# Two more token tiles kept in DRAM, and a fifth Strassen pair in the last stage of a fused attention and feed-forward kernel

## The chip, the cores and the metric

The kernel runs on one core of one Trainium2 chip. The metric is the device time of one execution in microseconds (us). A core has a matrix engine (PE, the tensor engine), a vector engine (VectorE, DVE in the profile), a scalar engine (ScalarE, ACT), GpSimd (POOL) and a queue engine (SP). PE reads from the on-chip memory SBUF and writes to PSUM, a small memory of eight banks that VectorE and ScalarE read. Transfers to and from DRAM are issued by SP, ACT and POOL, each in the order of its own queue. Every engine works through its queue in order, and waits at an instruction until the semaphores that it names have reached their values.

## The reference

```python
def _attn_ref(q, k, v):                      # q, k, v: 8 batches, 12 heads, 448 tokens, 64 wide
    scores = scale * np.matmul(q, k.transpose(0, 1, 3, 2))
    attn = np.maximum(scores, 0.0) ** 2 / S
    return np.matmul(attn, v)

def _moe_ref(x, g_ln, w_ch1, w_ch2):         # x: 8 batches, 448 tokens, 768 wide
    xn = (x - mu) / np.sqrt(var + 1e-06) * g_ln
    ch = np.maximum(xn @ w_ch1, 0.0) @ w_ch2   # 768 -> 3072 -> 768
    return x + ch
```

Scores are squared after the relu, not put through a softmax. The attention's output, with its heads side by side, is the x of the feed-forward part. The result is the residual x plus the second product, `ch`.

## The kernel before

**Pairs and stages.** The eight batches are taken two at a time: four pairs of 896 tokens, that is 7 tiles of 128 tokens each (t = 0 to 6). The code counts pairs from 0; this text calls them the first to the fourth, but keeps the code's number where it quotes the code. For each pair there is attention, a first product (768 to 3072, kept transposed in `hT`) and a second product (3072 to 768). The normalisation's scale per token (`rstd`) is applied behind the second product, which is linear in it.

The program alternates. The first product of pair p (`ffn1_pair`, `run`, L960) has PE to itself. Then comes a stretch in which the second product of pair p is mixed with the attention of pair p + 1. In the profile these mixed stretches are at about 100 to 175 us (pair 0's second product), 222 to 290 us (pair 1's, which this text calls the third pair's stretch where the attention in it belongs to the third pair) and 336 to 406 us (pair 2's; the fourth pair's stretch). The last stage, from 452 us, is pair 3's second product alone.

**Second product.** Directly (`ffn2`, L740), a tile takes 2 halves of 384 output columns x 24 matmuls = 48. By Strassen's scheme (`ffn2_pair`, L1099) two tiles of tokens, halves of the 3072 rows and halves of the 768 columns form 2 x 2 blocks, and 7 products of 12 matmuls do the work of 96. The sums of blocks of `h` are formed on VectorE (`h_sums_of`), the sums of blocks of `w2` (`t1`, `t3`, `t4`, `t6`, `t7`) on GpSimd and VectorE ahead of time. Pair 0 does 7 tiles directly. Pair 1 does 6 directly, in the order 0, 1, 2, 4, 5, 6, and keeps its middle tile, t = 3, in DRAM (`odd_out`, L789). Pair 2 does its own middle tile in `ffn2_mid` (48 matmuls) and three Strassen pairs, (0, 4), (1, 5) and (2, 6). Pair 3 does these three and a fourth, its middle tile with the one that pair 1 kept, which `odd_in` (L795) reads back into a free quarter of `w1`. The first Strassen pair of the last stage has a third PSUM bank (`third`), so that its products 4, 3 and 1 can start before the first product's last rows are there.

**The mixed stretches.** `interleave` (L13) runs a list of main units (parts of the second product: 6 matmuls each when direct) and a list of side units (attention), and spreads the second evenly over the first. A direct tile has 8 units, 4 for each half. The last part of a half calls `finish` (L754), which on VectorE (L756) takes the PSUM result, multiplies it by `rstd`, adds the residual tokens `xtok` (the buffer `xt_room`, one for all pairs) and writes one of three output buffers `o_room`. The store of one half is issued on SP (L776) when the next half finishes. Two units of pair 1 come ahead of the mixed list, and the last three behind the attention, so 43 of its 48 units are spread.

The side list (`attention`, L600) has 42 scores (6 groups of four heads x 7 blocks of 64 keys), three to a bundle: 14 bundles, one last value product, and two hooks. A score is 4 matmuls (L366), a relu on ScalarE (L377) into `attn_sb`, and a square, on VectorE (L381) or, for the third of a bundle in some stretches, on ScalarE (L379). There are three PSUM slots for scores and value products, and nine `attn_sb` buffers. The value product of a group (28 matmuls, L398) comes one or two bundles after the one with the group's last score, and VectorE scales it into `xT` (L404). After the last score of a group, SP issues the transposes of the keys and queries of the group three further on (L313, L318, L319), and POOL loads later ones.

The hook `even` stands tenth of the 17 side units. It issues on SP the fetches of the sums of `w1` that the next first product needs (L845), and, by the table `soon`, part of the transposes that put the next pair's attention output into `xt_room` as tokens:

```python
    soon = {(1, "even"): (0, 3, range(K1)), (2, "odd"): (0, 2, range(K1))}
```

that is, in pair 1's stretch token tiles 0 to 2, all 6 column blocks, one DMA transpose for each (`tokens_part`, L648). The remaining tiles, 3 to 6, follow beside the first product, in `between_two`.

**What orders it.** The program order is the order in which these Python functions run. A tracking layer places semaphores by it: a read of a buffer waits for the writes that stand ahead of it in the program, a write for the reads.

**Sums beside pair 1.** `beside_of` puts six VectorE additions (L1025, `t6` and `t7`) behind given main units.

Of the kernel before, what the change touches and what calls it, by code (L numbers as in the profile page):

```python
# [28 lines left out]
def kernel(  # L29
# [22 lines left out]
    nc = tc.nc  # L52
# [42 lines left out]
    odd_root = const.tile([P, 1], fp32)  # L95
# [162 lines left out]
    def transposes(b, m):  # L258
# [11 lines left out]
        if (b, m) == (0, 0):  # L270
# [5 lines left out]
            idle(32)  # L276
# [323 lines left out]
    def attention(bs, hooks):  # L600
# [25 lines left out]
        def bundle(items, at):  # L626
            for o, it in enumerate(items):
                item(*it, o == 2 and bs[0] in (by_dma, B - 2))
                if o == at:
                    product(it[0] - 1)  # L630
        units, due = [], [[]]
        for s in range(0, len(seq), 3):
            items = seq[s:s + 3]
            at = max((o for o, (n, i) in enumerate(items[:2]) if n > lo and i in (1, 2)), default=-1)
            units.append(lambda items=items, at=at: bundle(items, at))
# [149 lines left out]
    odd_kept = dram.tile([P, K2 + K1, P], bf16, name="odd_kept")  # L785
# [280 lines left out]
    def ffn2_mid(pair, a, b):  # L1066

        h = hT[pair].rearrange("p (kh k) s -> p kh k s", kh=2)[:, :, :, 3 * P:4 * P]  # L1070
        s, n = room0[:, :KH], KH - 1
        a, b = a[:, :DH], b[:, :DH]

        def rows(ps, left, name, lo, hi, first=False, last=False):
            for k in range(lo, hi):
                nc.tensor.matmul(ps, left[:, k], w2_sum[name][:, k], start=(first and k == lo),  # L1076
                                 stop=(last and k == hi - 1))

        def most(*at, **kw):
            rows(*at, 0, 6, **kw)  # L1080
            yield
            rows(*at, 6, n)
        yield from most(a, h[:, 1], "t4", first=True)
        nc.vector.tensor_add(s[:, :n], h[:, 0, :n], h[:, 1, :n])
        yield
        yield from most(b, h[:, 0], "t3", first=True)
        yield
        nc.vector.tensor_add(s[:, n], h[:, 0, n], h[:, 1, n])
        h_sums_of(pair, 0, "s1")
        for half, ps, left, name, then in ((0, a, h[:, 1], "t4", "t2"), (1, b, h[:, 0], "t3", "t5")):  # L1090
            if half:
                yield
            yield from most(ps, s, then)
            rows(ps, left, name, n, KH)
            rows(ps, s, then, n, KH, last=True)
            finish(pair, 3, half, 0, K1, ps, (nc.sync, nc.sync))
            h_sums_of(pair, 0, "s2", half * KQ * 2, (half + 1) * KQ * 2)

    def ffn2_pair(pair, t, ts, two_banks, z, last, third=None):  # L1099
# [3 lines left out]
        at, half = h_parts(pair, t), KH // 2  # L1103
# [20 lines left out]
        def result(ps, row, half):  # L1124
            p, u = (odd["pair"], MID) if t == MID and row else (pair, t + 4 * row)
            root = odd_root if p != pair else rstd[pair][:, u:u + 1]
            x = odd["x"] if p != pair else xtok[pair][:, :, u]
# [17 lines left out]
        else:  # L1145
# [20 lines left out]
            nc.vector.tensor_add(z, z, c)  # L1166
# [39 lines left out]
    def ffn2_units(pair):  # L1206
# [3 lines left out]
        if pair == 1:  # L1210
            then[order[-1]] = MID

        def unit(t, h, p):
            if h == 0 and p == 1 and t in then:
                statistics(pair, then[t])
# [200 lines left out]
```

## Time and profile before

| | us |
|---|---|
| median of 3 runs | 514.39 (514.38, 514.39, 516.76) |
| profiled execution | 513.95 |
| its span, first to last instruction | 512.2 |
| third pair's first product beside nothing else, 289.7 to 336.3 | 46.6, PE busy 46.6 |
| last stage, 459.2 to 512.2 | 53.0, PE busy 48.8, VectorE 33.8 |

| main groups by line | count | busy us |
|---|---|---|
| L745 second product, direct | 624 | 107.6 |
| L1114 second product, Strassen (all forms) | 588 | 103.6 |
| L1076 the middle tile of pair 2 | 48 | 9.0 |
| L377 relu of scores on ScalarE | 150 | 126.3 |
| L381 squares on VectorE | 98 | 60.0 |
| L379 squares on ScalarE | 28 | 26.6 |

A profile's span is the time from the first to the last instruction; the time of an execution is 1.75 us longer here. Busy times of PE overlap at the ends of matmuls (they are pipelined), so a group's mean duration is longer than the distance between its matmuls. "Idle before, releaser" is the time in which an engine had nothing to run and what ended it. SPq, ACTq and POOLq are the queues that issue transfers.

### The profile page before, as it was taken

Reading aid. Unit: us, or ns where it says so; the run is one execution under the profiler, and the core shown is the slowest. Engines: PE = TensorE matmul, PEld = TensorE weight load, DVE = VectorE, ACT = ScalarE, POOL = GpSimd, SP = SyncE. Lnnn points to the kernel's source line nnn. Section 1 sums busy time; section 2 is a strip of 40 time slices with the busy share of each in tenths; the row PEclk is TensorE's granted clock in tenths of the full one; section 3 lists DMA queues with packets and bytes.
Section 4 is the critical chain, followed back from the end, with each engine's and each line's share of the span. In section 5 each row is a group of like instructions: output and inputs, shape, how many; then the busy total and the mean of one; then the engine's idle time right before and its main releaser. Section 6 shows DMA issues by size and latency. Waiting matters only on the chain.

```text
span 512.2 us, 11457 instructions
## 1 busy us (share of the span) xinstructions
PE 504.7 (99%) x4559; PEld 299.7 (59%) x4559; DVE 385.0 (75%) x738; ACT 310.0 (61%) x513; POOL 130.3 (25%) x182
## 2 busy tenths in 40 slices
PE   8999999999999999999999999999999999999996
PEld 6677778955555555555555555555555555556663
DVE  4885755778787798858789968858887968868663
ACT  5966776588668266657757266639979366730000
POOL 8335102012402266321101099601100022200000
PEclk9999999999999999999999999999999999999999
DMA  9999999999979994329996999304997393322222
GB/s 198 206 207 206 210 206 157 157 149 211 167 134 193 173 226 139 129 66 175 186 234 111 196 177 185 93 11 79 185 193 174 75 219 117 94 77 63 63 61 61
DMA packets 124486, 76.31 MB, mean 149 GB/s; under 512 B 80562, under 2 KB 120498, under 8 KB 124434
## 3 DMA queue, kind: packets, MB, share of 16 engines
q1 hardware_dynamic: 93730, 41.38, 39.5%
q0 software_dynamic: 28544, 30.91, 37.4%
q10 hardware_dynamic: 2160, 3.31, 2.8%
q8 instruction: 35, 0.57, 0.5%
q14 instruction: 17, 0.14, 0.1%
HBM read 64.69 MB, written 17.89 MB: 161 GB/s over the span
## 4 chain that ended last, share of the span: by engine, by line
PE 95%; ACT 2%; DVE 2%; issue 0%; ACTq 0%
PE m_ps L903 28%; PE o_ps L745 19%; PE o_ps L1114 11%; PE m_ps L1114 8%; PE h_ps L686 8%; PE sc_ps L366 7%; PE av_ps L398 6%; PE h_ps L731 2%; ACT early L377 2%; PE h_ps L713 2%; PE o_ps L1076 2%; PE tr_ps L250 1%; PE idle_ps L236 1%; PE sum_ps L431 0%; DVE w L485 0%; ACT attn_sb L377 0%
## 5 line engine op out<-in xcount | busy, mean ns | idle before, releaser
L377 ACT ACTIVATE attn_sb<-sc_ps 128x896 bf16<-128x896 f32 (+4 forms) x150 | 126.3, 903 | 37.5 <-PE sc_ps L366 32.4
L907 ACT ACTIVATE hT_sb<-m_ps 128x448 bf16<-128x448 f32 x144 | 78.2, 543 | 52.1 <-PE m_ps L903 49.3
L745 PE MATMUL o_ps<-w,hT_sb 128*128 128x384 bf16 x624 | 107.6, 326 | 0.0
L745 PEld LDWEIGHTS <-hT_sb 128*128 128x128 bf16 x624 | 58.4, 98 | 46.0 <-issue 9.9
L381 DVE TENSOR_TENSOR attn_sb<-attn_sb 128x896 bf16<-128x896 bf16 x98 | 60.0, 622 | 25.0 <-ACT attn_sb L377 24.4
L686 PE MATMUL h_ps<-x_room,w 128*128 128x192 bf16 (+2 forms) x384 | 43.9, 263 | 0.0
L1114 PEld LDWEIGHTS <-hT_sb 128*128 128x128 bf16 x312 | 29.8, 98 | 22.0 <-issue 3.0
L985 DVE TENSOR_TENSOR m_ps<-x_room,m_ps 128x448 f32<-128x448 f32 x36 | 22.6, 628 | 21.6 <-ACT hT_sb L907 21.5
L686 PEld LDWEIGHTS <-w 128*128 128x128 bf16 x384 | 33.8, 97 | 6.9 <-issue 1.4
L903 PEld LDWEIGHTS <-w 128*128 128x128 bf16 x246 | 24.0, 97 | 22.8
L1114 PEld LDWEIGHTS <-x_room 128*128 128x128 bf16 x252 | 24.2, 98 | 17.3 <-issue 1.6
L404 DVE TENSOR_SCALAR xT_sb<-av_ps 128x896 bf16<-128x896 f32 (+2 forms) x30 | 27.0, 900 | 9.2 <-PE av_ps L398 8.9
L967 ACT COPY x_room<-m_ps 128x448 f32<-128x448 f32 x36 | 19.1, 531 | 21.2 <-PE m_ps L903 20.5
L903 PEld LDWEIGHTS <-w_sum 128*128 128x128 bf16 x210 | 20.5, 98 | 19.3 <-DVE w_sum L879 0.4
L159 POOL DMA_DIRECT2D k_sb<-in_k_dram x15 | 10.7, 713 | 79.6 <-DMA kT_sb<-k_sb 57.2
L159 POOL DMA_DIRECT2D v_sb<-in_v_dram x20 | 14.2, 710 | 58.6 <-PE sc_ps L366 44.2
L903 PE MATMUL m_ps<-x_sum,w 128*128 128x448 bf16 x120 | 29.1, 352 | 0.0
L663 DVE BATCH_NORM_STATS2 stats<-xtok_sb 128x6 f32<-128x384 bf16 x56 | 28.3, 547 | 0.9 <-DMA xtok_sb<-xT_sb 0.9
L366 PE MATMUL sc_ps<-qT_sb,kT_sb 64*64 64x448 bf16 x392 | 28.1, 358 | 0.2 <-ACT x_room L481 0.2
L485 DVE SCALAR_TENSOR_TENSOR w<-w,g_sb,x_room 128x512 bf16<-128x512 bf16 x36 | 25.6, 738 | 3.0 <-ACT x_room L481 3.0
L379 ACT ACTIVATE attn_sb<-attn_sb 128x896 bf16<-128x896 bf16 x28 | 26.6, 950 | 0.9
L398 PE MATMUL av_ps<-attn_sb,v_sb 64*64 64x448 bf16 (+2 forms) x532 | 26.1, 330 | 0.0
(196 smaller groups left out, 867.6 us busy)
## 6 DMA issues: line engine op xcount, KB each, us to landing
out_dram<-o_room SPq DMA_DIRECT2D x108, 96.0 KB, 2.5
w<-in_moe_w_ch_dram POOLq DMA_DIRECT2D x12, 384.0 KB, 14.1
w<-in_moe_w_ch_dram POOLq DMA_DIRECT2D x4, 1152.0 KB, 20.1
q_sb<-in_q_dram POOLq DMA_DIRECT2D x20, 224.0 KB, 5.9
v_sb<-in_v_dram POOLq DMA_DIRECT2D x20, 224.0 KB, 6.2
k_sb<-in_k_dram POOLq DMA_DIRECT2D x15, 224.0 KB, 5.3
kept<-room SPq DMA_DIRECT2D x4, 480.0 KB, 2.6
kept<-w_sum SPq DMA_DIRECT2D x16, 96.0 KB, 1.8
```

Source lines behind the costliest of these rows:

```text
L366: nc.tensor.matmul(ps[cols, r, o * w:(o + 1) * w], g["k"](i)[rows, cols], g["q"](i, r)[rows, blk[0]:sum(blk), cols], start=True, stop=True)
L377: nc.scalar.activation(a, ps[:, :, :len(slots) * w], ACTF.Relu)
L379: nc.scalar.activation(a, a, ACTF.Square)
L381: nc.vector.tensor_mul(a, a, a)
L398: nc.tensor.matmul(ps[cols, hh, :w], v_sb[rows, pr, j * D:(j + 1) * D], g["attn"][i][rows, r, :], start=(j == 0), stop=(j == J - 1))
L404: nc.vector.tensor_scalar_mul(x, ps[:, :, :w], score_scale)
L663: nc.vector.bn_stats(stats[:, n], xtok[pair][:, n * G:(n + 1) * G, t, :])
L686: nc.tensor.matmul(ps[:, :w + more], w1[:, c, ni * P:(ni + 1) * P], xc[b][:, c, s.start:s.stop + more], start=(c == 0), stop=(c == K1 - 1))
L745: nc.tensor.matmul(ps[:, :DH], hT[pair][:, ki, t * P:(t + 1) * P], w2[:, ki, cols], start=(o == 0), stop=(o == K2 - 1))
L903: nc.tensor.matmul(ps, *at, start=(first and c == 0), stop=(c == KQ - 1), skip_group_check=not first)
L907: nc.scalar.activation(hT[pair][:, n + KH * row, half * S:(half + 1) * S], ps, ACTF.Relu)
L1114: nc.tensor.matmul(ps, x[:, ki], y[ki] if isinstance(y, list) else y[:, ki], start=(first and ki == 0), stop=(ki == KH - 1), skip_group_ch ...
```

## The change

Two more tiles go the way of pair 1's middle tile. `LEFT` lists what is left to the last stage: of pair 1 the tiles 3 and 6, of pair 2 the tile 3. `odd_out` writes each, its `h` (24 x 128 columns) and its residual tokens, to a DRAM buffer of its own; `odd_roots` copies its `rstd` column. `odd_in` reads all three back in the last stage: into two free quarters of `w1` and into the `xT` of the last pair. Pair 1 now does five tiles directly: 0, 1, 2, 4, 5. `ffn2_mid` is gone; pair 2's stretch has the three Strassen pairs alone, the first with a third bank as in the last stage. Pair 3 has five Strassen pairs, the fifth made of pair 1's tile 6 and pair 2's tile 3. Further, which third scores of a bundle are squared on ScalarE is now given by `squares`: beside pair 0 all (as before), beside pair 1 those of every third bundle (before: none), beside pair 2 those of two bundles in three (before: all). The six additions beside pair 1 stand behind other units, and two idle matmuls at the start are left out. The table `soon` and the hooks are as before.

```diff
-            idle(32)
+            idle(30)
...
+        squares = {by_dma: (0, 1, 2), by_dma + 2: (0,), B - 2: (0, 1)}.get(bs[0], ())
+
-        def bundle(items, at):
+        def bundle(items, at, turn):
             for o, it in enumerate(items):
-                item(*it, o == 2 and bs[0] in (by_dma, B - 2))
+                item(*it, o == 2 and turn in squares)
...
+    LEFT = ((1, MID), (1, NT - 1), (2, MID))
...
     def odd_out(pair):
-        nc.gpsimd.dma_start(odd_kept[:, :K2], hT[pair][:, :, MID * P:(MID + 1) * P])
-        nc.gpsimd.dma_start(odd_kept[:, K2:], xt_room[:, :, MID])
-        odd["pair"] = pair
+        for i, (p, u) in enumerate(LEFT):
+            if p == pair:
+                nc.gpsimd.dma_start(odd_kept[i][:, :K2], hT[pair][:, :, u * P:(u + 1) * P])
+                nc.gpsimd.dma_start(odd_kept[i][:, K2:], xt_room[:, :, u])
...
     def odd_in():
-        t = w1[:, :KQ, :KH * P].rearrange("p c (k s) -> p c k s", s=P)
-        nc.sync.dma_start(t[:, :2].rearrange("p c k s -> p c (k s)"),
-                          odd_kept[:, :K2].rearrange("p (c k) s -> p c (k s)", c=2))
-        nc.sync.dma_start(t[:, 2, :K1], odd_kept[:, K2:])
-        odd["h"], odd["x"] = t[:, :2], t[:, 2, :K1]
+        x = xT[B // 2 - 1].rearrange("p c s -> p (c s)")[:, :(K2 + K1) * P].rearrange("p (c s) -> p c s", s=P)
+        for i, room in enumerate((w1[:, :KQ, :KH * P], w1[:, KQ:, KH * P:], None)):
...
+            nc.sync.dma_start(to.rearrange("p c k s -> p c (k s)"),
+                              odd_kept[i][:, :K2].rearrange("p (c k) s -> p c (k s)", c=2))
+            nc.sync.dma_start(odd[i]["x"], odd_kept[i][:, K2:])
...
     def h_parts(pair, t):
-        two = [h[:, :, :, t], odd["h"] if t == MID else h[:, :, :, t + 4]]
+        if t > MID:
+            two = [odd[1]["h"], odd[2]["h"]]
+        else:
+            two = [h[:, :, :, t], odd[0]["h"] if t == MID else h[:, :, :, t + 4]]
...
     def ffn2_units(pair):
-        order = [t for t in range(NT) if pair != 1 or t != MID]
-        then = dict(zip(order, order[1:]))
-        if pair == 1:
-            then[order[-1]] = MID
+        others = [u for p, u in LEFT if p == pair]
+        order = [t for t in range(NT) if t not in others]
+        then = {t: [u] for t, u in zip(order, order[1:])}
+        then[order[-1]] = others
...
     def strassen_units(pair, mm, banks, third=None):
         def all_of():
             end = pair == pairs - 1
-            if not end:
-                yield from ffn2_mid(pair, *mm)
-            for t in range(MID + end):
-                yield from ffn2_pair(pair, t, MID + end, banks(t), zs[t % 2], end and t == MID,
+            ts = MID + 2 * end
+            for t in range(ts):
+                yield from ffn2_pair(pair, t, ts, banks(t), zs[t % 2], end and t == ts - 1,
                                      third if t == 0 else None)
             yield
         g = all_of()
-        return [lambda: next(g)] * 4, [lambda: next(g)] * (4 + 3 * 14), g
+        return [lambda: next(g)] * 4, [lambda: next(g)] * (9 + 2 * 14), g
...
-            head, units, _ = strassen_units(pair, mm, lambda t: mm[::-1] if t % 2 else mm)
+            third = ps_m.tile([P, 512], fp32, tag="m", name="m_ps")
+            head, units, _ = strassen_units(pair, mm, lambda t: mm[::-1] if t % 2 else mm, third)
...
-            if pair == 1:
-                odd_out(pair)
+            odd_out(pair)
+            if last:
+                units.pop(0)()
+                odd_roots(pair)
...
-            units = beside_of(units, dict(zip((10, 17, 24, 34, 36, 39), sums)))
+            units = beside_of(units, dict(zip((9, 15, 21, 27, 31, 34), sums)))
```

More of the change, by code (lines that the diff above doesn't have):

```diff
@@ L634, in attention @@
             at = max((o for o, (n, i) in enumerate(items[:2]) if n > lo and i in (1, 2)), default=-1)
-            units.append(lambda items=items, at=at: bundle(items, at))
+            units.append(lambda items=items, at=at, s=s: bundle(items, at, s // 3 % 3))
             n = items[at][0] - 1
@@ L1064, in h_sums_of @@
             nc.vector.tensor_sub(a[0, 1], a[0, 1], a[1, 1])
[L1066 to L1097, printed above, removed]
     def ffn2_pair(pair, t, ts, two_banks, z, last, third=None):
-        at, half = h_parts(pair, t), KH // 2
+        at, half, s1 = h_parts(pair, t), KH // 2, h_sum["s1"]
+        if third is not None and pair < B // 2 - 1:
+            h_sum["s1"] = room0[:, :KH]
         left = dict(h_sum, s3=at[0, 0], s4=at[1, 1], s6=at[1, 0], s7=at[0, 1])
@@ L1207, in ffn2_units @@
         rows = late_rows(K2)
[L1208 to L1211 removed]
+        others = [u for p, u in LEFT if p == pair]
+        order = [t for t in range(NT) if t not in others]
+        then = {t: [u] for t, u in zip(order, order[1:])}
+        then[order[-1]] = others
         def unit(t, h, p):
[L1214 to L1219 removed]
+            if h == 0 and p == 1:
+                for u in then[t]:
+                    statistics(pair, u)
+            if h == 1 and p == 2:
+                for u in then[t]:
+                    roots(pair, u, u + 1)
+                if t == order[-1]:
+                    odd_roots(pair)
             ffn2(pair, t, h, p, rows=rows)
```

27 lines of the change are left out of this document (18 added, 9 removed).

## The prediction

> **What bounds the kernel now.** I read the busy shares first, then the chain that ended last, then the stretches beside attention, and last the queues by order of time. Page, busy time and chain by engine:
>
> ```profile
> PE 504.7 (99%) x4559; PEld 299.7 (59%) x4559; DVE 385.0 (75%) x738; ACT 310.0 (61%) x513; POOL 130.3 (25%) x182
> PE 95%; ACT 2%; DVE 2%; issue 0%; ACTq 0%
> ```
>
> TensorE is busy all the time, and its matmuls are 95% of the chain. Whatever leaves them saves its own length, as long as no other queue makes PE wait. Nothing does so now: PE's waits are 3.2 us in all, and none lies behind 141 us. The two stretches that lose a tile, by engine (length, then busy us of PE, PEld, DVE, ACT, POOL, clock, DMA share, GB/s):
>
> ```profile
> 228.20:289.70 61.50, 61.50 (x597) 32.91 (x597) 50.87 (x91) 37.15 (x48) 8.76 (x13) 1.00 1.08 182
> 344.10:405.70 61.60, 61.60 (x597) 33.20 (x597) 50.78 (x80) 49.68 (x59) 5.03 (x7) 1.00 0.77 143
> ```
>
> PE is full, VectorE at 83%, DMA full in the first. The chain in order of time gives PE's unit prices (start, us):
>
> ```profile
> 254.61 1.32 PE av_ps L398 x28
> 256.13 2.06 PE o_ps L745 x12
> 258.18 0.69 PE sc_ps L366 x12
> 258.87 4.98 PE o_ps L745 x30
> ```
>
> A second-product matmul (384 columns) takes 0.1625 us (18 of them between 12 and 30 differ by 2.92); a group of them after scores costs 0.11 more; three scores 0.69; a value product with its three scores 2.09.
>
> The third view is SP's queue beside the third pair's second product (start, us in issuing):
>
> ```profile
> 252.65 1.31 SPq L313 DMA_TRANSPOSE kT_sb<-spare  x1
> 254.07 1.76 SPq L318 DMA_TRANSPOSE qT_sb<-q_sb  x1
> 255.88 2.02 SPq L319 DMA_TRANSPOSE qT_sb<-q_sb  x1
> 257.99 2.50 SPq L776 DMA_DIRECT2D out_dram<-o_room  x4
> 260.54 1.07 SPq L845 DMA_DIRECT2D room<-kept  x2
> 261.66 3.83 SPq L845 DMA_DIRECT2D w<-kept  x4
> 265.53 8.46 SPq L648 DMA_TRANSPOSE xtok_sb<-xT_sb  x6
> ```
>
> SP works without a break here. The six L648 transposes overwrite token tiles 0 to 2 with the next pair's tokens; the last starts at 272.7 and lands 2.4 us later (the six: 2.4 to 4.6). VectorE's queue at that time:
>
> ```profile
> 257.78 0.61 DVE L381 TENSOR_TENSOR attn_sb<-attn_sb 128x896 bf16<-128x896 bf16 x1
> 258.31 0.61 DVE L756 SCALAR_TENSOR_TENSOR o_room<-o_ps,rstd_sb,xtok_sb 128x384 f32<-128x384 f32 x1
> ```
>
> The L756 at 258.31 is the second half of tile 2, the last reader of those tiles: 7 us before the transposes start.
>
> **The change part by part.** *Matmuls.* Removed: two tiles done directly, 2 x 48. Added: a fifth Strassen pair, 7 x 12 = 84. That is 12 fewer, 12 x 0.1625 = -1.95 us. Each stretch loses 48 (7.8 us), and the last stage gains 84 (13.65 us).
>
> *Two idle matmuls less.*
>
> ```profile
> 1.09 3.59 PE L236 MATMUL idle_ps<-ones 128*128 128x128 bf16 x32 [1.09 <-DVE ones L98]
> ```
>
> 3.59 / 32 = 0.112 us each. The query cast ends at 4.23 and the keys' first at 4.65, so the transposes behind can move up: -0.2 (bounds -0.22 and 0).
>
> *The hook with the six transposes.* It stands tenth of 17 attention units, spread over all but three of the second product's units. With 43 such units it came after the 26th (with two ahead, 28 of 48, so tiles 0, 1, 2 were done). With 35 it comes after the 21st: 23 with the two ahead, and tile 2's second half ends in the 24th. The transposed range is still tiles 0 to 2. So the transposes now stand ahead of that half's result in the program's order: SP must wait for tile 2's first half, and VectorE's result of the second half must wait until all six have landed (its addend is then what they wrote). Behind it on VectorE stand the t6 sum and the square of the first scores of the tenth bundle, and PE's value product of the same group of heads (the fourth) reads that square.
>
> When does PE get there? From 225.3 by the unit prices, with 18, then nine times 12, then 24 matmuls between the attention groups: tile 2's first half ends at 253.4, its second at 258.2, and the value product has used all it has at 263.1.
>
> When do the six land? SP has four stores fewer ahead. Its three key and query transposes wait for scores that PE now reaches earlier: the second set starts at about 241.6 (fifth bundle) and takes 6.5 as now, the store pair 1.25, the third set 249.4 to 254.7, stores to 256.0, the six fetches of kept sums 4.9 as now, to 261.0. The six then need 7.2 to the start of the last and 2.4 to land: 270.6. VectorE then does the result, the sum and the square (0.53 + 0.87 + 0.62, by the spacing of such rows), 272.6. PE's early stall below puts its arrival at 263.5, so it waits 9.1; if a landing counts from the end of its issue, 10.4. I take **+9.5**. Lower bound: every SP row at its shortest (transposes 1.25, stores 0.6, fetches 0.43) gives a last landing at 265.6 and a wait of 4. Upper bound: the new writes (next) slow SP and the landings by 4 us, 13.5.
>
> *After that wait.* VectorE has some 5 us of squares, statistics and results queued, and PE restarts from 9 us of idleness. For such a restart the nearest row is the kernel's start, 0.112 for 128 columns against 0.1625 / 3 = 0.054 later, which is 1.8 us over 32 matmuls; if it doesn't apply, VectorE's queue makes the next value product but one wait some 1.2. The two overlap: **+1.5** (0 to 2.5). [...]
>
> *Writes to DRAM.* One tile costs 0.96 MB on POOL's queue (226.2 to 235.9 now), and 1.46 + 0.84 us of POOL. The added tile in the third pair's stretch pushes the key and query loads behind it from landing at 238.8 to some 247; their transposes are due at 249.4. The one in the fourth pair's stretch lies where DMA has room (0.77). Both hidden; without that slack the third set and all behind it slip, which is the upper bound above.
>
> *Squares.* Five go to ScalarE in the third pair's stretch, four return to VectorE in the fourth's: 0.95 and 0.62 each. Scores have three PSUM slots, so a bundle's third score waits for the third relu of the bundle before. Where 12 matmuls lie between, a bundle comes each 2.75; ScalarE takes 2.54, with a square 3.49. Third pair's stretch: one such place near its start, **+0.45** (0 to 1).
>
> Fourth pair's stretch: two of three bundles carry a square, seven of thirteen gaps are 2.75 and five 4.15, one 4.7. Working forward, relus fall behind 0.65, 0.15, 0.25, 0.3, 0.3 and with the two z copies (0.47) some 0.3: 2. VectorE does 50.8 + 4.0 in 69.4 now; less the mid tile (0.88 + 0.23 + 2 x 0.61), plus 2.5 for squares and 0.6 for split sums, 55.6 in 61.6, so a value product's slot comes free about 0.7 late once. **+2.5** (0.5 to 5).
>
> *Hidden.* The first products in three banks, as in the last stage now (no wait of PE there). Three reloads instead of one, some 14 us at 4.7 each, ahead of the stores: the fourth result would find its buffer 1.7 late, which the next pair's three products (5.85 us) cover. The fifth pair's sums: VectorE has 33.8 in 53 there.
>
> Sum on the profiled execution (513.95, span 512.2 and 1.75 around it): -1.95 - 0.2 + 0.45 + 9.5 + 1.5 + 2.5 = +11.8, so 525.75. The median 514.39 is 0.44 above that execution; I say **526**.
>
> **The rivals.** *Not slower: the transposes hide.* PE loses nothing if the square is ready at 263.5, so if the last transpose lands by 261.5. SP would have to start them at 251.9. Against: they wait for tile 2's first half, which PE ends at 253.4 and VectorE later, and SP is behind. For: all times on SP after this point are extrapolated, and a PE that is late itself shortens the wait. Then 513.95 - 2.15 + 0.5 to 2.5 = 512.3 to 514.3. Chance 0.05.
>
> *The wait is there but short.* SP catches up, since most of its backlog is DMA pressure: wait 4, little behind it, 518 to 522. Speaks for it: sets of three take 3.9 where DMA is free (275.4 on). 0.2.
>
> *More than that.* DMA is full and gets 0.96 MB more in less time, or VectorE at 90% holds PE in the fourth pair's stretch by 5: 530 to 535. 0.17.
>
> *The change doesn't do what it says.* The order of instructions shows the 12 matmuls gone, so only the squares' part could fail: in the sums' bounds.
>
> **How the numbers follow.** My own case (523 to 529.5) has 0.56, and 0.02 is for none of these. The range 518 to 532 leaves out the hidden case and most of the larger one's tail. A measurement here can't tell less than about 0.5% (2.6 us) from no change. The hidden case saves at most 2.15, so it falls within that: faster 0.02, same 0.06, slower 0.92.
>
> **What would show it.** In the changed profile: an idle of VectorE of some 10 us before the result in the third pair's stretch, released by the DMA of xtok_sb from xT_sb; an idle of PE of 7 to 12 us inside a value product at about 263, released by a square on VectorE; short PE waits on ScalarE or VectorE in the fourth pair's stretch, 2 to 3 us in all; 336 matmuls in one piece at the end, and no PE wait there. It is wrong if PE is still without waits in the third pair's stretch, or if the wait sits elsewhere.

## The result and the profile after

The changed kernel takes 540.86 us (median of 5 runs, 538.1 to 542.35), the kernel before 514.39 beside it: ratio 1.048, interval 1.0446 to 1.0523. The profiled execution took 540.86, its span is 539.1, 26.9 us above the span before. Forecast were 526 us, 518 to 532.

The page of the changed kernel, busy times, chain by engine:

```profile
PE 510.7 (95%) x4545; PEld 301.0 (56%) x4545; DVE 390.2 (72%) x750; ACT 310.8 (58%) x515; POOL 134.9 (25%) x186
...
PE 72%; DMA 11%; ACT 6%; DVE 6%; issue 2%; SPq 1%; POOL 1%; ACTq 0%; DVEq 0%
```

PE has 14 instructions fewer and is busy 6 us longer: some of its matmuls ran slowly. Of the chain, which was 95% PE's, 11% is now DMA. Line numbers are those of each kernel: L747, L758, L650, L918 and L1040 of the changed kernel are L745, L756, L648, L903 and L1025 of the kernel before. PE's longest waits in the changed kernel (total us, times, longest; `m_ps` is the first product's result in PSUM):

```profile
PE av_ps L398 <- DVE attn_sb L381: 11.6, 1, 11.6
PE sc_ps L366 <- DMA qT_sb<-q_sb: 4.0, 1, 4.0
PE sc_ps L366 <- ACT attn_sb L377: 1.7, 5, 0.5
PE m_ps L918 <- DVE x_room L984: 1.2, 2, 0.7
...
PE m_ps L918 <- DVE xT_sb L404: 0.8, 1, 0.8
```

The first is the wait that the prediction named, the second none that it named. Where they lie shows PE's timeline (start, us, instruction, then in brackets the idle time before it and what ended it):

```profile
256.16 0.96 PE L366 MATMUL sc_ps<-qT_sb,kT_sb 64*64 64x448 bf16 x8 [4.02 <-DMA qT_sb<-q_sb]
...
260.04 2.86 PE L747 MATMUL o_ps<-w,hT_sb 128*128 128x384 bf16 x12
...
268.22 2.12 PE L747 MATMUL o_ps<-w,hT_sb 128*128 128x384 bf16 x12
...
283.38 0.96 PE L398 MATMUL av_ps<-attn_sb,spare 64*64 64x448 bf16 x7 [11.60 <-DVE attn_sb L381]
...
285.02 4.01 PE L747 MATMUL o_ps<-w,hT_sb 128*128 128x384 bf16 x12
```

Twelve matmuls of the second product take 2.12 us. Behind the idle of 4.0 us they take 2.86, behind that of 11.6 us 4.01. Stretches of 5 us of the changed kernel (length, busy us of PE, PEld, DVE, ACT, POOL, then PE's granted clock, DMA share, GB/s) say why:

```profile
253.00:258.00 5.00, 1.84 (x21) 1.07 (x24) 1.35 (x4) 1.48 (x3) 1.40 (x2) 0.67 1.17 158
258.00:263.00 5.00, 5.00 (x40) 2.33 (x36) 3.33 (x5) 1.44 (x2) 0.70 (x1) 0.64 1.28 232
...
278.00:283.00 5.00, 0.00 (x0) 0.00 (x0) 1.69 (x3) 0.00 (x0) 0.00 (x0) 0.50 0.36 79
283.00:288.00 5.00, 4.62 (x25) 2.11 (x25) 4.97 (x10) 1.73 (x2) 1.23 (x2) 0.50 0.88 174
```

In both places the clock falls to 0.50 while PE idles and stays low for some microseconds after it, to 262 and to 289 us: each wait is paid for a second time. Against the same groups at their usual pace, what follows the 4.0 us takes 2.6 us longer (256.16 to 262.83), and what follows the 11.6 us takes 2.7 longer (283.38 to 288.95). The 11.6 us are what VectorE's queue passes on, as forecast; its timeline has the result of tile 2's second half waiting for the next pair's tokens, which the program order puts ahead of it. They overwrite the residual of that half, so the changed kernel adds the next pair's tokens to it:

```profile
281.31 0.62 DVE L758 SCALAR_TENSOR_TENSOR o_room<-o_ps,rstd_sb,xtok_sb 128x384 f32<-128x384 f32 x1 [14.02 <-DMA xtok_sb<-xT_sb]
```

The 4.0 us come from SP's queue. The first set of key and query transposes in the kernel before:

```profile
235.09 1.27 SPq L313 DMA_TRANSPOSE kT_sb<-k_sb  x1
236.44 1.75 SPq L318 DMA_TRANSPOSE qT_sb<-q_sb  x1
238.25 1.29 SPq L319 DMA_TRANSPOSE qT_sb<-q_sb  x1
```

and in the changed kernel, down to the six token transposes:

```profile
235.25 2.40 SPq L313 DMA_TRANSPOSE kT_sb<-k_sb  x1
237.75 7.83 SPq L318 DMA_TRANSPOSE qT_sb<-q_sb  x1
245.63 3.85 SPq L319 DMA_TRANSPOSE qT_sb<-q_sb  x1
...
272.34 7.71 SPq L650 DMA_TRANSPOSE xtok_sb<-xT_sb  x6
```

The first three begin at the same time as before, but issuing them takes 14.1 us instead of 4.3. POOL has just issued two writes of `odd_kept` where there was one (227.35 to 231.87), and the chain of the changed kernel runs through the second (start, us):

```profile
231.04 13.29 DMA odd_kept<-xtok_sb
...
245.63 10.40 DMA qT_sb<-q_sb
...
256.16 0.96 PE sc_ps L366 x6
```

The stages of the profiled executions up to e10, from the starts of PE's groups (us; "start" is where the direct second product begins, "3rd" the third pair's stretch, "1st" the first product behind it, "4th" the fourth pair's stretch, "last" the last stage to the end of the span; the fourth pair's first product takes 46.5 to 46.9 in all). "Planned" is before with the matmuls moved: 48 x 0.1625 = 7.8 less in two stretches, 13.65 more at the end.

| kernel | start | 3rd | 1st | 4th | last | span |
|---|---|---|---|---|---|---|
| before | 222.1 | 67.4 | 46.7 | 69.4 | 60.1 | 512.2 |
| planned | 222.1 | 59.6 | 46.7 | 61.6 | 73.8 | 510.2 |
| changed | 223.2 | 82.6 | 48.6 | 64.3 | 73.8 | 539.1 |
| e1 two tiles transposed | 222.6 | 68.8 | 48.8 | 64.0 | 73.7 | 524.5 |
| e7 one write, three tiles | 222.5 | 74.9 | 47.6 | 64.9 | 73.8 | 530.2 |
| e6 one write, two tiles | 222.5 | 62.0 | 47.9 | 64.9 | 73.8 | 517.5 |
| e10 write in long pieces | 222.9 | 64.1 | 49.0 | 64.9 | 73.8 | 521.3 |
| e4 write late | 223.6 | 62.0 | 54.1 | 64.0 | 73.8 | 524.0 |
| e5 write in the middle | 222.5 | 62.0 | 47.6 | 64.0 | 73.8 | 516.5 |
| e8 e5, squares dealt otherwise | 222.2 | 60.3 | 48.4 | 63.6 | 73.8 | 515.1 |
| e9 e8, sums and statistics moved | 222.3 | 63.6 | 50.1 | 64.4 | 73.8 | 520.6 |
| e2 before with the token wait | 222.1 | 74.9 | 46.9 | 69.4 | 60.1 | 519.9 |
| e3 before with a second write | 222.3 | 71.6 | 47.5 | 69.4 | 60.1 | 517.4 |

Of the 28.9 us between planned and changed, 23.0 lie in the third pair's stretch: waits of 4.0, 0.4, 11.6 and 0.8, and the low clock behind the two long ones, 5.3 us; that makes 22.1. The last stage is as planned.

### The profile page after: what moved, and what is told of

It is laid out like the page before. It is cut to its first block, busy times and chain, and to the rows that moved or that the text cites. A ratio compares the mean times of both kernels' runs of the same rounds, so it can differ in the third digit from the quotient of the medians.

```text
span 539.1 us, 11471 instructions
## 1 busy us (share of the span) xinstructions
PE 510.7 (95%) x4545; PEld 301.0 (56%) x4545; DVE 390.2 (72%) x750; ACT 310.8 (58%) x515; POOL 134.9 (25%) x186
## 4 chain that ended last, share of the span: by engine, by line
PE 72%; DMA 11%; ACT 6%; DVE 6%; issue 2%; SPq 1%; POOL 1%; ACTq 0%; DVEq 0%
PE m_ps L918 25%; PE m_ps L1101 11%; PE o_ps L747 10%; PE o_ps L1101 7%; PE h_ps L688 7%; DMA xtok_sb<-xT_sb 5%; PE sc_ps L366 5%; PE av_ps L398 4%; ACT attn_sb L377 3%; DMA odd_kept<-xtok_sb 2%; DMA qT_sb<-q_sb 2%; ACT early L377 2%; PE h_ps L715 1%; SPq L650 1%; DMA out_dram<-o_room 1%
## 5 line engine op out<-in xcount | busy, mean ns | idle before, releaser
L747 PE MATMUL o_ps<-w,hT_sb 128*128 128x384 bf16 x576 | 102.4, 333 | 0.0
L747 PEld LDWEIGHTS <-hT_sb 128*128 128x128 bf16 x576 | 54.5, 99 | 44.9 <-issue 12.7
L381 DVE TENSOR_TENSOR attn_sb<-attn_sb 128x896 bf16<-128x896 bf16 x97 | 59.6, 623 | 26.3 <-ACT attn_sb L377 25.6
L1101 PEld LDWEIGHTS <-hT_sb 128*128 128x128 bf16 x312 | 29.9, 98 | 21.4 <-issue 2.1
L918 PEld LDWEIGHTS <-w 128*128 128x128 bf16 x246 | 24.0, 97 | 24.3 <-issue 1.9
L1101 PEld LDWEIGHTS <-x_room 128*128 128x128 bf16 x276 | 26.4, 98 | 19.2 <-issue 2.2
L366 PE MATMUL sc_ps<-qT_sb,kT_sb 64*64 64x448 bf16 x392 | 29.7, 366 | 6.2 <-DMA qT_sb<-q_sb 4.0
L404 DVE TENSOR_SCALAR xT_sb<-av_ps 128x896 bf16<-128x896 f32 (+2 forms) x30 | 27.0, 901 | 9.2 <-PE av_ps L398 9.0
L918 PEld LDWEIGHTS <-w_sum 128*128 128x128 bf16 x210 | 20.4, 98 | 20.0 <-DMA w_sum<-kept 0.9
L918 PE MATMUL m_ps<-x_sum,w 128*128 128x448 bf16 x120 | 29.0, 352 | 1.2 <-DVE x_room L984 1.2
L398 PE MATMUL av_ps<-attn_sb,v_sb 64*64 64x448 bf16 (+2 forms) x532 | 27.5, 343 | 0.0
L1101 PE MATMUL m_ps<-w,x_room 128*128 128x384 bf16 x156 | 27.2, 327 | 0.0
```

Source lines behind the costliest of these rows:

```text
L366: nc.tensor.matmul(ps[cols, r, o * w:(o + 1) * w], g["k"](i)[rows, cols], g["q"](i, r)[rows, blk[0]:sum(blk), cols], start=True, stop=True)
L381: nc.vector.tensor_mul(a, a, a)
L398: nc.tensor.matmul(ps[cols, hh, :w], v_sb[rows, pr, j * D:(j + 1) * D], g["attn"][i][rows, r, :], start=(j == 0), stop=(j == J - 1))
L404: nc.vector.tensor_scalar_mul(x, ps[:, :, :w], score_scale)
L747: nc.tensor.matmul(ps[:, :DH], hT[pair][:, ki, t * P:(t + 1) * P], w2[:, ki, cols], start=(o == 0), stop=(o == K2 - 1))
L918: nc.tensor.matmul(ps, *at, start=(first and c == 0), stop=(c == KQ - 1), skip_group_check=not first)
```

## The experiments

The question after the result was how many costs there are: the wait for the tokens and the second write, each on its own with its slow clock; or one, a stretch with too much DMA work for its length, in which whatever is freed in one place is lost in the next. The letters of the expectations are theirs. Times are medians, ratios to the kernel before on the same chip; the kernel before took 514.4 to 515.0 us in all of them.

**e1: two tiles transposed.** In the changed kernel, the hook takes tokens 0 and 1 only; tile 2 follows in the next first product.

```diff
-            tokens_part(2, 3, NT, (n,))
-        if n > 2 and side["tokens"]:
+            tokens_part(2, 2, NT, (n,))
+        if n > 3 and side["tokens"]:
...
-    soon = {(1, "even"): (0, 3, range(K1)), (2, "odd"): (0, 2, range(K1))}
+    soon = {(1, "even"): (0, 2, range(K1)), (2, "odd"): (0, 2, range(K1))}
```

> The changed kernel with the early transposes cut to token tiles 0 and 1; tile 2 goes with the late ones beside the first product, whose statistics start one block later. Theory A (VectorE's result behind six transposes): the 14.0 us wait of VectorE and the 11.6 us wait of PE go, and with them the 2.8 us of halved clock behind it, so 540.9 - 14.4 = 526.5; the 4.0 us wait for the query transposes at 252 stays. Rival C (attention with less second product beside it is bound by ScalarE or VectorE, whatever the order): 535 or more, with PE waiting for squares or relus in many places.

526.56 us, ratio 1.0228 (1.0204 to 1.0252): 14 us of the loss are gone with one token tile less. PE's waits in this kernel:

```profile
PE sc_ps L366 <- DMA qT_sb<-q_sb: 4.1, 1, 4.1
PE m_ps L918 <- DVE xT_sb L404: 2.3, 1, 2.3
```

The value product's wait is gone, that for the query transposes is as large as it was: they are two costs.

**e2: the token wait alone, in the kernel before.** Pair 1's tiles are taken in the order 0, 1, 4, 2, 5, 6, so that tile 2's second half comes behind the hook (its residual is then what the transposes wrote, as in the changed kernel).

```diff
-        order = [t for t in range(NT) if pair != 1 or t != MID]
+        order = [0, 1, 4, 2, 5, 6] if pair == 1 else list(range(NT))
...
```

> The kernel before, with the direct tiles of pair 1 in the order 0, 1, 4, 2, 5, 6, so that tile 2 is under way when the hook comes, and nothing else; the residual of its second half is then what the transposes wrote. Theory A: the same wait appears without any of the change: VectorE waits some 10 us for the transposes, PE 7 to 10 at the value product behind 268, 1 to 3 for the restart: 523 to 527. Rival C: no less second product, so 514.4.

522.62 us, ratio 1.0158 (1.0129 to 1.0188), just under the 523 to 527 expected. VectorE's and PE's timelines of this kernel:

```profile
274.11 0.62 DVE L756 SCALAR_TENSOR_TENSOR o_room<-o_ps,rstd_sb,xtok_sb 128x384 f32<-128x384 f32 x1 [6.64 <-DMA xtok_sb<-xT_sb]
```

```profile
276.31 0.96 PE L366 MATMUL sc_ps<-spare 64*64 64x448 bf16 x8 [4.61 <-DVE xT_sb L404]
...
277.57 5.36 PE L745 MATMUL o_ps<-w,hT_sb 128*128 128x384 bf16 x18
```

VectorE waits at the same result for the same transposes. It gets there at 267.5, as in the changed kernel (267.3), but waits less, since SP issues the six transposes from 264.6 on and not from 272.3. PE idles 4.6 us, not inside the value product as expected but at the scores behind the next second-product group, for L404. Its stretch is 7.5 longer: 18 matmuls that take 3.10 elsewhere in this stretch take 5.36 behind the wait, at a clock of 0.50 (277 to 282 us). No write was added, so this slow clock is the wait's alone.

**e3: the write alone, in the kernel before.** Pair 1's last tile is also written to a DRAM buffer that nothing reads.

```diff
...
+        nc.gpsimd.dma_start(more_kept[:, :K2], hT[pair][:, :, (NT - 1) * P:])
+        nc.gpsimd.dma_start(more_kept[:, K2:], xt_room[:, :, NT - 1])
```

> The kernel before, which also writes pair 1's tile 6 (h and residual) to a DRAM buffer that nothing reads. Theory B (the second write fills the DMA engines and delays the first set of query transposes): these land at 256 as in the changed kernel, where PE needs them at 254.1 here: a PE wait of 1 to 2 us, under what halves the clock: 515.5 to 517. If writes are hidden, as predicted: 514.4.

519.05 us, ratio 1.0089 (1.0069 to 1.0109): 4.7 us, more than was expected either way. The first query transpose on SP's queue in this kernel:

```profile
237.79 6.12 SPq L318 DMA_TRANSPOSE qT_sb<-q_sb  x1
```

With nothing else changed, it takes 6.1 us to issue instead of 1.75. PE doesn't wait for this transpose here, as it needs the scores later. The cost comes by way of SP's queue, where the stores of results stand behind the transposes. VectorE's and PE's waits in this kernel, one row of each:

```profile
DVE o_room L756 <- DMA out_dram<-o_room: 4.7, 2, 4.0
```

```profile
PE av_ps L398 <- DVE attn_sb L381: 1.7, 1, 1.7
```

VectorE waits up to 4.0 us for an output buffer that hasn't been stored yet, and PE 1.7 us for the square behind that result. That 1 to 2 us are under what halves the clock was an estimate: the changed kernel's rows still read 1.00 at 1.9 us into the idle of 4.0 and at 3.2 us into that of 11.6, but here the 27 matmuls behind the 1.7 us take 1.76 us, 0.4 over their usual pace; whether the clock fell is not shown. A further 1.7 (L404) and 0.6 us (L972) follow where the next first product starts. Even the kernel before had no room for this write at this place.

**e4: the write late.** As e1, but tile 6 is written at the second hook.

```diff
...
-            if p == pair:
+            if p == pair and late == (i == 1):
...
             following[name]()
+            if (pair, name) == (1, "odd"):
+                odd_out(1, True)
```

> e1 with the write of pair 1's tile 6 moved from the start of the stretch to the second hook, near its end. Theory B: the 4.0 us wait for query transposes and the 3.3 us of halved clock behind it go: e1 less 7.3, about 519. If the writes are not the cause (density, rival C): as e1.

525.18 us, ratio 1.0203 (1.0185 to 1.0222). The stretch falls from 68.8 to 62.0 us, and the next first product grows from 48.8 to 54.1. ScalarE's and PE's timelines of this kernel:

```profile
295.04 0.98 ACT L922 ACTIVATE hT_sb<-m_ps 128x448 bf16<-128x448 f32 x2 [8.11 <-DMA odd_kept<-hT_sb]
```

```profile
296.30 1.28 PE L918 MATMUL m_ps<-x_sum,room 128*128 128x448 bf16 x3 [5.15 <-DVE m_ps L1000]
```

The write, issued at 281.5, reads `hT` until 295; the next first product's relus overwrite `hT` and wait for it, and PE with them. The cost only moved, and the time that was expected was missed by 6 us.

**e5, e6, e7: the write in the middle; no second write.** e5 is e4 with the write at the first hook:

```diff
-            if (pair, name) == (1, "odd"):
+            if (pair, name) == (1, "even"):
```

e6 (from e1) and e7 (from the changed kernel) leave the second write out:

```diff
-            if p == pair:
+            if p == pair and i != 1:
...
-                              odd_kept[i][:, :K2].rearrange("p (c k) s -> p c (k s)", c=2))
+                              odd_kept[(0, 0, 2)[i]][:, :K2].rearrange("p (c k) s -> p c (k s)", c=2))
...
```

> As the kernel with the late write (525.18 us), but the third pair's last tile goes to DRAM at the first hook, in the middle of the stretch, ahead of the token transposes, when the DMA rows so far show a gap behind it (share 0.27 and 0.61 at 275 to 285). Theory A, the second write costs only through what it stands ahead of: neither the query transposes (4.1 us of PE wait and 1.7 of slow clock when early) nor the next pair's relus (5.2 us and 1.5 when late) wait for it, so 525.18 - 6.7 = 518.5 us. Theory B, the shortened stretch has no room for 0.96 MB more on the DMA engines: the wait only moves again, to the token transposes and the statistics behind them, and the time stays at 523 us or above.

> As the kernel with two transposed token tiles (526.56 us), but the third pair's last tile is not written to DRAM; the last stage reads the odd tile's kept data in its place, so one tile's output is another's. This is the change without its second write and without the wait for the tokens. By my sum the writes were hidden, so it should stay near 526.56 us. If the second write makes the query transposes late, the 4.1 us of wait and 1.7 of slow clock go: 520.7 us. If VectorE's waits at the stretch's end (2.3, 1.1 and 0.7 us) come from it too: 517 us.

> As the changed kernel (540.86 us), transposing three token tiles, but without the second write, as in the run before. My sum took the writes as hidden; if nothing but the write was mis-sized, this kernel is the one that the sum describes: 526 us, with a PE wait of 9.5 us at the value product. If the write cost only its own 4.0 us of wait and 3.3 of slow clock: 533.5 us, with the value product's wait still at 11.6 us.

| | three tiles transposed | two |
|---|---|---|
| two writes, both early | 540.86 (changed kernel) | 526.56 (e1) |
| one write | 531.95 (e7), ratio 1.0275 to 1.0394 | 519.08 (e6), 1.0063 to 1.0105 |
| two writes, one in the middle | not tried | 519.95 (e5), 1.0074 to 1.0148 |

The write costs 8.9 us in one column and 7.5 in the other, the token wait 14.3 and 12.9 in the two rows. e7's four runs lie between 528.4 and 536.2, so the 8.9 and the 12.9 are known to some 3 us only. Within that the two costs are additive: e6 and e7 came out 1.6 us under the 520.7 and 533.5 that were expected if the write has its price. And e5, with all bytes written, is within 1 us of e6, without them. SP's queue in e5, its first query transpose and the token transposes:

```profile
236.30 2.83 SPq L318 DMA_TRANSPOSE qT_sb<-q_sb  x1
...
262.96 9.85 SPq L650 DMA_TRANSPOSE xtok_sb<-xT_sb  x6
```

The query transpose is quick again (2.99 in e6, without the write). The write now slows the token transposes (9.85 us, 7.63 in e6), for which in this kernel PE does not wait. A of e5's expectation holds, 1.5 us over its time: the write's price is that of what it stands ahead of. e7 is the kernel that the prediction's sum describes, with the write taken out of play; PE's timeline of it:

```profile
275.58 0.96 PE L398 MATMUL av_ps<-attn_sb,spare 64*64 64x448 bf16 x7 [10.88 <-DVE attn_sb L381]
...
277.22 3.37 PE L747 MATMUL o_ps<-w,hT_sb 128*128 128x384 bf16 x12
```

**e10: the same bytes in long pieces.** e1's second write takes its 768 KB from one run of 6144 bytes per partition, not from 24 pieces of 256.

```diff
+                if i == 1:
+                    piece = (hT[pair].rearrange("p c s -> p (c s)")[:, :K2 * P]
+                             .rearrange("p (c s) -> p c s", s=P))
...
```

> As the kernel with two transposed token tiles (526.56 us), its second write at the same place and of the same bytes, but the 768 KB of hidden values are taken from one stretch of 6144 bytes per partition instead of 24 pieces of 256 bytes, so one tile's output is computed from other hidden values. If the write holds up the query transposes by its many small pieces, most of its 7.5 us go: 520 us. If by its bytes on full DMA engines, it stays at 526.5 us with the 4.1 us of PE wait.

522.61 us, ratio 1.0141 (1.0121 to 1.0162): between the two, 4 us under e1 and 3.5 over e6. The first query transpose on SP's queue in this kernel:

```profile
237.74 3.94 SPq L318 DMA_TRANSPOSE qT_sb<-q_sb  x1
```

With the kernel's L313 and L319 of that set, issuing takes 9.2 us, against 14.2 with small pieces (e1) and 5.9 in e5. Both the pieces and the bytes cost here, about half each (POOL also issues the long pieces sooner, in 0.56 us instead of 1.42). No run here measures the transfer rate alone.

**e8, e9, e11: what is left.** e5 is still 5.2 us above the kernel before beside it (514.74), which the 12 matmuls alone would have brought to 512.8. e8 gives ScalarE's squares in the third pair's stretch to other bundles, and in the fourth's to half as many:

```diff
-        squares = {by_dma: (0, 1, 2), by_dma + 2: (0,), B - 2: (0, 1)}.get(bs[0], ())
+        squares = {by_dma: range(14), by_dma + 2: (3, 6, 9, 12, 13), B - 2: (0, 3, 6, 9, 12)}.get(bs[0], ())
...
-            units.append(lambda items=items, at=at, s=s: bundle(items, at, s // 3 % 3))
+            units.append(lambda items=items, at=at, s=s: bundle(items, at, s // 3))
```

> As the kernel with the write in the middle, but the squares are dealt out otherwise: in the third pair's stretch ScalarE takes those of bundles 4, 7, 10, 13 and 14 (instead of 1, 4, 7, 10, 13), in the fourth pair's stretch five of fourteen (1, 4, 7, 10, 13) instead of ten. If ScalarE is what lengthens the fourth pair's stretch (64.04 us against 61.6 planned), it falls to 62 us or less and the time by 2 us; if VectorE is, which has some 56 us to do in 61.6, it stays or grows by 1 to 3 us. At the end of the third pair's stretch the waits for VectorE (0.8 and 0.7 us) fall by half a us.

518.1 us, ratio 1.0085 (1.0056 to 1.0114). The third pair's stretch falls by 1.7, to 0.7 over planned; the first product behind it grows by 0.8, and the fourth pair's stretch falls by only 0.4: halving ScalarE's squares there was not the remedy. With its interval the gain over e5 is not shown. PE's waits in e8, from 222 to 400 us:

```profile
PE sc_ps L366 <- ACT attn_sb L377: 1.3, 4, 0.5
PE m_ps L918 <- DVE x_room L984: 1.0, 2, 0.8
PE m_ps L918 <- ACT x_room L982: 0.6, 1, 0.6
```

e9 moves VectorE's sums and the kept tiles' statistics to where VectorE had idle time, and the squares again:

```diff
-            units = beside_of(units, dict(zip((9, 15, 21, 27, 31, 34), sums)))
+            units = beside_of(units, dict(zip((2, 5, 8, 27, 28, 29), sums)))
...
-        then[order[-1]] = others
+        then[order[-1]] = []
+        for t, u in zip(order[1:], others):
+            then[t].append(u)
...
```

> As the kernel with the squares dealt out otherwise (518.1 us, span 515.1), with VectorE's work spread: the sums t6 and t7 after units 3, 6, 9, 28, 29, 30 instead of 10, 16, 22, 28, 32, 35 of the third pair's stretch, the statistics of the two kept tiles earlier than its last tile, and ScalarE's squares in both stretches in bundles 2, 4, 6, 10, 12, 14, which stand ahead of a value product. If VectorE's late work is what makes the next first products slow (48.36 us against 46.67 before), they fall to 47 us and the fourth pair's stretch (63.60) to 63: 516 us. Should every wait of the two stretches go, the 12 matmuls fewer would show: 512.5 us. If the lost time is in the grouping of the matmuls and not in waits, 518 us.

522.08 us, ratio 1.014 (1.0123 to 1.0157): worse than e8 by 4, and than each of the three times expected. PE's and VectorE's timelines of this kernel:

```profile
242.85 0.57 PE L366 MATMUL sc_ps<-spare 64*64 64x448 bf16 x8 [2.03 <-DVE xT_sb L404]
```

```profile
239.23 0.96 DVE L665 BATCH_NORM_STATS2 stats<-xtok_sb 128x6 f32<-128x384 bf16 x2
...
240.35 0.91 DVE L1040 TENSOR_TENSOR w<-w 128x1536 bf16<-128x1536 bf16 x1
...
241.71 1.08 DVE L404 TENSOR_SCALAR xT_sb<-av_ps 128x896 bf16<-128x896 f32 x1
```

Statistics and a sum now stand in front of the L404 that empties a value product's PSUM slot, and the next score waits for that slot. e11 takes e8 and moves only the last two sums, to units 30 and 32.

```diff
-            units = beside_of(units, dict(zip((9, 15, 21, 27, 31, 34), sums)))
+            units = beside_of(units, dict(zip((9, 15, 21, 27, 29, 31), sums)))
```

> As the kernel with the squares dealt out otherwise (518.1 us, span 515.1), with the last two t7 sums four and three units earlier, where VectorE had short idle times. If VectorE's late work alone lengthens the next first products (48.36 us against 46.67 before), they come to 47.3 us and the time to 517 us; if the sums push back the eviction of a value product, as in the run before, 519 us or more. The floor, should nothing wait at all, is 512.4 us.

521.83 us, ratio 1.0103 (1.0067 to 1.014), with runs from 517.0 to 524.9. In its profiled execution the first product comes down to 47.5 us, near what was expected of it, but the stretch starts at 225.7. PE's timeline at the kernel's start, first of e11:

```profile
8.86 0.71 PE L341 MATMUL busy_ps<-ones 128*128 128x128 bf16 x5
```

and of the changed kernel:

```profile
7.69 0.45 PE L341 MATMUL busy_ps<-ones 128*128 128x128 bf16 x5
```

These five matmuls are the same ones in both. In e11 the array is at a slow pace there (0.71 us for 0.45), though the granted clock in its rows from 4 to 16 us is 1.00.

**e12 to e15: the two idle matmuls.** I took the two that the change leaves out for the cause of this, and of the wide spread. e12 is e11, e14 the changed kernel, e15 is e8, each with `idle(32)` again; e13 is the kernel before with `idle(30)`.

> As the kernel with the early t7 sums (runs of 517.0 and 517.1, and of 519.7 to 524.9 us), with 32 idle matmuls at the start as before instead of 30. In that kernel's profile the five busy matmuls at 8.86 still take 0.71 us (0.45 at 7.69 in the changed kernel's), and the third pair's stretch begins at 225.7 instead of 222.2. If the two idle matmuls left out are what lets the array stay slow in some runs, the spread goes and all runs lie near 516.5 us. If the spread is of another origin, a third or more of the runs stay at 520 us and above.

> The kernel before with 30 idle matmuls at the start instead of 32, nothing else. My sum gave this part of the change -0.2 us: 514.2 us, runs as close together as before (513.8 to 516.1). If the shorter warm-up leaves the array slow for longer in some runs: runs at 514 and runs at 517.5 to 519 us.

> The changed kernel (540.86 us; runs 538.1 to 542.35) with 32 idle matmuls as before. If the start adds up to 3.5 us in some runs only: 538.3 us with little spread. If not: 540.9 us as it was.

> The kernel with the squares dealt out otherwise (518.1 us; six runs of 516.7 to 518.7, four of 520.9 to 522.5) with 32 idle matmuls. If the start is the cause of the spread: all runs at 516.5 to 517.5 us; if not, 518 us with the same two groups.

e12: 519.64 us, 516.8 to 523.2, the spread as wide as e11's. e13: 515.13, 513.8 to 518.0, ratio 1.001 (0.9991 to 1.0028). e15: 518.08, 516.6 to 521.5, as e8. So the two matmuls are neither a gain nor a loss that can be measured, and this theory fell. e14 came to 537.82 (four runs of 536.3 to 538.1, and one of 738.0 that stands in no ratio), ratio 1.0432 (1.0409 to 1.0456), for the most part below the changed kernel's 1.0446 to 1.0523. But in its profile most of the difference is in the third pair's stretch (79.0 for 82.6), 200 us and more behind the two matmuls, so the start can't be named as its cause. There PE waits 2.9 us for the query transposes instead of 4.0, and no slow time follows (8 scores in 0.57 us, for 0.96); the token wait is 1.0 longer, and the slow time behind it 0.8 shorter. Together that is the difference; why the first wait was shorter is not shown. What lets these kernels vary by 5 us from run to run stays open.

No version beat the kernel before. The most that the change could win is its 12 matmuls, 1.95 us.

## Why the prediction was wrong

*Right: the token wait.* It is at the place, on the line and through the two queues that the prediction named, and its bounds held: 11.6 us in the changed kernel, 10.9 in e7, for 9.5 (4 to 13.5). In e7 both its ends are near the prediction's: PE arrives at 264.7 (263.5), VectorE goes on at 273.5 (the last landing at 270.6). In the changed kernel both ends are 8 to 11 us late, 271.8 and 281.3, and that the difference stayed was luck. *What follows it* was forecast as +1.5 (0 to 2.5). It is 2.0 in e7 (12.9 for wait and aftermath, e7 less e6, with a wait of 10.9) and 2.7 in the changed kernel, just over the bound. The prediction left the choice between VectorE's backlog and a slow array open. The clock rows (0.50 from 283 to 288 us) and e2's 5.36 us for 3.10 show the slow array. The 1.8 us for it were an estimate from the kernel's first matmuls, where the clock reads 1.00 (0 to 10 us of the kernel before); that those are slow for the same reason is not shown.

*Wrong: "Both hidden".* This is the step that failed. The prediction saw that the added write makes what is behind it late, and looked only at the loads on POOL's own queue, which had slack until the third set of transposes. The transposes of the first set are on SP's queue, and the page counts all queues on the same 16 DMA engines, which the prediction's view had shown full (a share of 1.08); these transposes were already due, and PE reached their scores at 252. The write's price is 7.5 to 8.9 us (e1 less e6, the changed kernel less e7). In the changed kernel 4.0 of it are wait, 2.6 the slow clock behind it (not the 3.3 of e4's and e7's expectations), and 1.3 a token wait that is 0.7 longer with 0.6 more of slow clock; the rest lies outside the stretch. The other write, in the fourth pair's stretch, is in every version of the change; PE waits for no transfer there in the changed kernel, and 0.6 and 0.7 us in e6 and e7. The rival "More than that" named this cause (full DMA gets 0.96 MB more in less time), gave it 0.17, and priced it at 4 to 9 us over the sum, which is what the write alone cost. The time lies above the rival's 535 since the rest of the sum was too low as well: e7, without the write, takes 531.95 us for 526.

*Right: matmuls; in size only: the fourth pair's stretch.* The last stage is 13.7 longer (13.65). The fourth pair's stretch is 64.3, 2.7 over planned (+2.5). But PE's waits there, four of 0.2 to 0.5 for ScalarE and one of 0.3 for VectorE, are 1.6 us together and not 2 to 3, so 1.1 of the 2.7 is not explained. The remedy that the forecast suggested, fewer squares on ScalarE, brought 0.4 (e8): the cause is only partly shown, and the match of the sizes is in part luck. ScalarE's early wait in the third pair's stretch is 0.42 (+0.45).

*Left out: VectorE at the end of the third pair's stretch.* The sum ended the stretch's costs with the stretch. With both large costs gone, e6 still has the stretch 2.4 over planned (+0.45 was forecast) and the first product behind it 1.2 over: PE's start there waits 0.8 us for VectorE's L404, then 0.7 for L984, the first product's own first sum. That, with a fourth pair's stretch 3.3 over planned in e6 for the +2.5, is most of why e6 is at 519.1 and not at 515, the sum without the token wait. *Two idle matmuls:* -0.2 was forecast, nothing was measured (e13).

In medians the loss of 26.5 us splits into 4.3 (e6 over the kernel before), 12.9 (token wait) and 8.9 (write). Along this path the parts must add up; that they are two costs is shown by the other path, through e1, with 7.5 and 14.3.

## What to carry to other kernels

A transfer is not hidden because nobody waits for its own data: ask which transfers of other queues it meets on the DMA engines, when theirs are due, and what stands behind them in their queue (in e3, the stores whose buffers VectorE needs: a wait of up to 4.0 us there, and 4.7 us of time). If the engines are full there, move it behind the last one that is due (e5: 519.95 us, for 526.56 in e1); but also look at who must overwrite what it reads (e4: 5.15 us of PE wait).

When a stage gets shorter, everything placed by position in it moves: a hook that is tied to a share of the units can pass a reader that it used to follow. Moving one token tile out of the hook (e1) was worth more than half of the loss (14.3 of 26.5 us).

Where PE is full, price a wait as wait plus slow restart: here 1.3 us (e4, a wait of 5.15) to 2.8 us (e2, a wait of 4.61) behind waits of 4.0 to 12.6 us, not growing with the wait, and nothing behind e14's 2.9. The two waits here didn't hide each other: the write cost 7.5 us without the token wait and 8.9 with it.

## What the runs showed of the hardware

The clock of PE fell to 0.50 after much shorter idles than the 11.6 us. In the changed kernel's rows of 1 us it falls 2 to 3 us into the idle of 4.0 us (0.87 from 254 to 255), is 0.50 from 255 to 261 and 1.00 again from 262 on. After 4.6 us in e2, 18 matmuls lost 2.3 us (0.50 from 277 to 282). In e10, 2.37 us of idle were enough (it falls just after PE has started again: 0.83 from 287 to 288, 0.50 from 288 to 290); in e14, 2.86 us were not, by the pace behind them (8 score matmuls take 0.57 us, not the 0.96 of the slow pace). PE's timeline of e10, where 6 matmuls take 1.80 us for 1.30 in e1:

```profile
287.02 1.80 PE L922 MATMUL m_ps<-xT_sb,room 128*128 128x448 bf16 x6 [2.37 <-DVE xT_sb L404]
```

and of e14:

```profile
254.73 0.57 PE L366 MATMUL sc_ps<-qT_sb,kT_sb 64*64 64x448 bf16 x8 [2.86 <-DMA qT_sb<-q_sb]
```

So at 2.4 to 2.9 us the length of the idle alone doesn't decide whether PE restarts slowly; what does is not shown.

A write of 0.96 MB from SBUF raised the time in which SP issues one DMA transpose from 1.75 us to 6.1 in e3, 7.8 in the changed kernel and 7.9 in e1, on another queue, at a DMA share (235 to 245 us) that was 1.22 in the kernel before and 1.13 in the changed one. The share alone didn't tell this; the duration of the issuing rows did.
